# Placing rows of x with TensorE, shorter k/r loads, spread constants, and a new order in a planned RWKV + gated MLP kernel

## The chip, the cores and the metric

The kernel runs on one core of one Trainium2 chip. The metric is the device time of one execution in microseconds (us). A core has TensorE (PE in the rows, its weight loads PEld), VectorE (DVE), ScalarE (ACT), GpSimd (POOL) and SyncE (SP), which here only issues DMAs.

## The reference

Per batch b (4), head h (8) and step t (768), with a head dimension of 48, a recurrence runs over the sequence, and its output feeds a gated MLP:

```
y[t]  = r[t] · (state + u * k[t] v[t]^T)
state = w[t] * state + k[t] v[t]^T
x = y, heads side by side: [4, 768, 384]
h = gelu(x @ w_in)              # 1024 wide: u = first 512, v = last 512
vn = (v - mean) / sqrt(var + 1e-6) * g_ln
vs = w_sg @ vn + b_sg           # over the 768 positions
out = x + (u * vs) @ w_out
```

All inputs are float32 but w_in and w_out, which arrive as float64.

## The kernel before

**Chunks.** The recurrence is cut into 24 chunks of 128 positions (6 per batch). For a chunk the kernel loads w (`load_w`), k and r in one tile KR (`load_kr`, 128 rows: two heads' 48 values each followed by 16 zero rows) and v (`load_v`). VectorE forms decays by two scans (`decays`, L485 and L490) and scales k and r (L514, L492). TensorE turns k (`turned_k`, L564), forms products of k, r and v (`products`, L579 and L582) and the outputs (`outputs`, L662 and L686). For the first six chunks the weights of a position on itself come from k times r (L524) and a small product (L528); later chunks load k and r a second time (`load_rk`) and use u spread over 128 rows (`u_bc`).

**x.** `outputs` copies y from PSUM into a tile x of four blocks [128, 384 positions per half sequence]. Blocks 0 to 2 are the 384 channels, but their rows 48 to 63 and 112 to 127 are empty at first: what belongs there lies in block 3. `move` carries it over with six small DMAs (two row groups by three blocks), for each chunk of the first batch and for a whole half elsewhere. `split_x` (L732 to L747) then writes x as the sum of two fp32r values, high and low: a cast for high, and for the low part either two products with an identity and a negative identity (L741, L742; the first two chunks, `ON_PE["x"]`) or a subtraction (L747).

**MLP.** Every matmul of the MLP is three fp32r products, high by high, high by low and low by high (L752 to L754). `v_piece` makes one chunk's v half of the hidden layer and normalizes it, `u_piece` a block of the u half for half a sequence, `gate_piece` the product with w_sg, `out_piece` the product with w_out, to which x is added (L850). The weights are split into high and low at the start: w_in in six pieces of 512 columns and w_out in four, by integer operations on VectorE (L874 to L882) and, for the first seven pieces, three products on TensorE (L887 to L889); w_sg in twelve pieces. The v pieces' weights are loaded first.

**Constants.** `consts` and `consts2` load u and b_sg with one DMA each that repeats the row over 128 partitions (L930, L936), and g_ln.

**Order.** Nothing is ordered at run time: each engine works through its own queue. The order of the queues is written by `Plan`, a list scheduler that runs while the kernel is built. Each `Op` carries a time per engine, the buffers it takes and frees, and the events it waits for; a DMA is costed by its kilobytes at 330 per us plus latencies. Of the operations that could start earliest on an engine the one with the lowest rank goes first; ranks stand in the tables `STEP`, `V`, `U`, `GATE`, `OUT`, `WEIGHT`, `EARLY`, `TILE`, `FIRST_LOADS`. Where the plan sees TensorE idle before its own time 36 (`WARM`), `keep_warm` (L991 to L1003) writes filler products into TensorE's queue, on a PSUM buffer that is free (L1002). They compute nothing that is used. All DMAs are issued by SP, in the order of the plan. Four PSUM buffers (`m_ps`) serve all products but those of the recurrence.

Of the kernel before, what the change touches and what calls it, by code (L numbers as in the profile page):

```python
# [21 lines left out]
C = 128  # L22
# [16 lines left out]
    38.78, 112.06, 158.75, 217.03, 62.66, 89.53, 134.81, 139.48, 142.68, 149.58, 150.62, 159.84, 162.31, 175.3,  # L39
    189.24, 197.8, 225.35, 212.87, 229.84, 236.4, 243.5, 266.54, 268.81, 362.79)  # L40
V = (
    107.75, 107.47, 46.81, -26.28, 63.79, 120.64, 133.54, 30.66, 190.17, 124.94, 47.43, 157.65, 120.92, 201.53,
    236.16, 159.51, 215.39, 298.31, 336.14, 50.73, 98.98, -9.56, 143.54, 156.75)
U = (17.13, 69.41, 298.46, 126.23, 235.77, -73.97, 85.66, 164.91)
GATE = (3.13, 142.62, 180.86, 144.47, 416.44, 288.73, 96.21, 162.36)
OUT = (267.68, 215.31, 231.79, 361.17, 600.9, 507.76, 441.48, 512.53)
WEIGHT = {"sg0": 131.6, "sg1": 102.52, "g": 182.31}

EARLY = {
    (0, 'decays'): -87.78, (0, 'range_check'): -6.74, (0, 'decayed_k'): -84.86, (0, 'turned_k'): 41.54,  # L50
    (0, 'own_weights'): 6.03, (0, 'first_products'): -46.25, (0, 'masked'): -12.48, (0, 'state'): -1.43,
    (0, 'outputs'): 38.84, (0, 'move'): -112.32, (0, 'split_x'): 9.34, (1, 'load_v'): 16.43,
    (1, 'decays'): 43.75, (1, 'range_check'): 8.92, (1, 'chunk_pc'): 39.98, (1, 'decayed_k'): 40.21,
    (1, 'turned_k'): 155.78, (1, 'own_weights'): 178.83, (1, 'first_products'): 18.08, (1, 'masked'): 26.68,
    (1, 'state'): 49.55, (1, 'decayed'): 41.46, (1, 'outputs'): -69.91, (1, 'move'): 72.17,
    (1, 'split_x'): 93.29, (2, 'load_w'): -38.11, (2, 'load_kr'): 19.39, (2, 'load_v'): 15.43,
    (2, 'decays'): 20.66, (2, 'range_check'): 72.63, (2, 'chunk_pc'): 61.08, (2, 'decayed_k'): 14.48,
    (2, 'turned_k'): 66.7, (2, 'own_weights'): 45.16, (2, 'first_products'): 119.93, (2, 'masked'): -47.19,
    (2, 'state'): 37.82, (2, 'decayed'): 152.85, (2, 'outputs'): 63.08, (2, 'move'): -39.02,
    (2, 'split_x'): 2.22, (3, 'load_w'): -57.23, (3, 'load_kr'): 65.19, (3, 'load_v'): 34.19,  # L60
    (3, 'decays'): 43.95, (3, 'range_check'): 82.06, (3, 'chunk_pc'): 20.23, (3, 'decayed_k'): 2.24,
    (3, 'turned_k'): 81.99, (3, 'own_weights'): 81.71, (3, 'first_products'): 60.11, (3, 'masked'): 69.15,
    (3, 'state'): 78.73, (3, 'decayed'): -34.21, (3, 'outputs'): 74.88, (3, 'move'): -8.38,
    (3, 'split_x'): -27.28, (4, 'load_w'): 69.55, (4, 'load_kr'): 61.22, (4, 'load_v'): 55.55,
    (4, 'decays'): 64.09, (4, 'range_check'): -7.16, (4, 'chunk_pc'): 3.0, (4, 'decayed_k'): 74.78,
    (4, 'turned_k'): -73.87, (4, 'own_weights'): 68.61, (4, 'first_products'): 37.28, (4, 'masked'): 39.48,
    (4, 'state'): 18.01, (4, 'decayed'): 58.71, (4, 'outputs'): 6.26, (4, 'move'): 133.34,
    (4, 'split_x'): -21.7, (5, 'load_w'): 71.5, (5, 'load_kr'): 108.33, (5, 'load_v'): 77.82,
    (5, 'decays'): 76.05, (5, 'range_check'): -19.43, (5, 'chunk_pc'): -118.45, (5, 'decayed_k'): 20.91,
    (5, 'turned_k'): 25.59, (5, 'own_weights'): 84.06, (5, 'first_products'): 32.76, (5, 'masked'): -74.99,  # L70
    (5, 'state'): -36.68, (5, 'decayed'): -134.86, (5, 'outputs'): -48.1, (5, 'move'): 56.59,
    (5, 'split_x'): 45.72}
TILE = {
    "v0": 13.86, "v1": 19.16, "v2": 13.59, "u0": -42.11, "u1": -123.0, "u2": -146.53, "out0": -148.91,
    "out1": 54.2, "out2": 2.98, "out3": -71.18}

HINTED = (mybir.EngineType.PE, mybir.EngineType.DVE, mybir.EngineType.SP)
BIAS = {"DVE": 0.09, "ACT": -0.33, "POOL": 0.08}
# [4 lines left out]
    (0, 'load_w'): -122.73, (0, 'load_kr'): -103.33, (1, 'load_w'): -96.72, (1, 'load_kr'): 8.17,  # L83
    (0, 'load_v'): -79.88}
# [91 lines left out]
class Plan:  # L176
# [20 lines left out]

    def add(self, rank, gen):
# [40 lines left out]
    def run(self):  # L239
        while True:  # L240
            best = {}
            for p in self.procs:
                op = p[3]
                if any(e.t is None for e in op.after) or any(len(s.free) < op.take.count(s) for s in op.take):
# [3 lines left out]
                              for s in (max([ready, self.engines[e], self.port if op.port(e) else 0.0, p[2].on(e)]  # L248
# [83 lines left out]
def rwkv_gmlp(ctx: ExitStack, tc: tile.TileContext, wpad, kr, vtok, ktok, vt, u, ucol, w_in, g_ln, w_sgT, b_sg, w_out, out):  # L332
# [16 lines left out]
    ident = cp.tile([128, 128], F32, name="ident")  # L349
# [24 lines left out]
    s_v = slots("vtok", 3, [DM + 16])  # L374
# [26 lines left out]
    minus, same = (per.tile([128, 128], F32R, name=x) for x in ("minus", "same"))  # L401
# [11 lines left out]
    nc.gpsimd.memset(full, 1.0)  # L413
    nc.gpsimd.affine_select(before, full, pattern=[[1, 128]], compare_op=ALU.is_gt, fill=0.0, base=0,
                            channel_multiplier=-1)
    make_identity(nc, ident)
# [6 lines left out]
    nc.scalar.copy(same, ident)  # L423
    for _, t in s_S2.free:
        nc.gpsimd.memset(t, 0.0)
    for _, t in s_v.free:
        nc.gpsimd.memset(t[:, DM:], 0.0)
# [16 lines left out]
    def dma(kb, **kw):  # L444
        return Op({"SP": 0.6 if kb == 10 else 0.45}, kb=kb, **kw)


# [7 lines left out]
    def load_kr(n):  # L455
        b, g = steps[n]
        op = yield dma(512, take=[s_kr], slack=1.5 if n > 1 else 0.5, done=ch[n].e_KR)
        ch[n].kr, = op.got
        ch[n].kr.n = 3
        ch[n].KR = ch[n].kr.tile  # L460
        nc.sync.dma_start(ch[n].KR, kr[b, g])

    def load_v(n):
        b, g = steps[n]
        op = yield dma(192, take=[s_v], slack=2.0, done=ch[n].e_V)
        ch[n].v, = op.got
# [103 lines left out]
    def products(n, op):  # L570
# [9 lines left out]
        for p, c_, j in [(p, c_, j) for p in range(NP) for c_ in range(1 if last else 2) for j in range(2)]:  # L580
# [3 lines left out]
                             x.V[64 * c_:64 * c_ + 64, h * D:(h + 1) * D], start=True, stop=True)  # L584
# [65 lines left out]
    def outputs(n):  # L650
# [545 lines left out]
```

## Time and profile before

| | |
|---|---|
| median of 3 runs | 361.15 us (360.0 to 362.67) |
| profiled execution | 360.76 us, span of the trace 358.9 us |
| TensorE busy | 347.7 us, 97% of the span, 4606 products |
| VectorE, ScalarE, GpSimd busy | 274.9, 211.4, 75.8 us |
| granted TensorE clock | 0.999 |
| moved by DMA | 49.79 MB, mean 139 GB/s |

The span runs from the first to the last instruction of the core. An engine's busy time is the time in which the profile shows it at work; matmuls overlap one another, so that the durations of single ones add up to more than the engine's time, and the chain of waits, which counts each moment once, gives what one of them takes from the next. A filler product counts as busy like any other. A DMA's time to landing runs from its issue to its arrival.

### The profile page before, as it was taken

Reading aid. Unit: us, or ns where it says so; the run is one execution under the profiler, and the core shown is the slowest. Engines: PE = TensorE matmul, PEld = TensorE weight load, DVE = VectorE, ACT = ScalarE, POOL = GpSimd, SP = SyncE. Lnnn points to the kernel's source line nnn. Section 1 sums busy time; section 2 is a strip of 40 time slices with the busy share of each in tenths; the row PEclk is TensorE's granted clock in tenths of the full one; section 3 lists DMA queues with packets and bytes.
Section 4 is the critical chain, followed back from the end, with each engine's and each line's share of the span. In section 5 each row is a group of like instructions: output and inputs, shape, how many; then the busy total and the mean of one; then the engine's idle time right before and its main releaser. Section 6 shows DMA issues by size and latency. Waiting matters only on the chain.

```text
span 358.9 us, 11141 instructions
## 1 busy us (share of the span) xinstructions
PE 347.7 (97%) x4606; PEld 320.8 (89%) x4606; DVE 274.9 (77%) x540; ACT 211.4 (59%) x564; POOL 75.8 (21%) x100
## 2 busy tenths in 40 slices
PE   6999998999999999999999999999899999999995
PEld 6978777899899989899999899989799988999994
DVE  7899898799999999999989988756942426545352
ACT  4887886793545588776423747685553588811010
POOL 3412141114238122241423110023100003200000
PEclk9999999999999999999999999999999999999999
DMA  7777875450266655743063266024415460000101
GB/s 246 290 218 217 262 224 186 145 193 4 89 204 212 202 170 202 233 150 117 7 221 129 89 221 198 1 71 131 152 59 163 134 200 1 23 24 22 46 22 71
DMA packets 23959, 49.79 MB, mean 139 GB/s; under 512 B 3808, under 2 KB 12768, under 8 KB 23904
## 3 DMA queue, kind: packets, MB, share of 16 engines
q1 hardware_dynamic: 23904, 49.04, 42.2%
q8 instruction: 37, 0.61, 0.7%
q14 instruction: 18, 0.15, 0.1%
HBM read 43.12 MB, written 4.72 MB: 133 GB/s over the span
## 4 chain that ended last, share of the span: by engine, by line
PE 85%; DVE 8%; issue 2%; ACT 2%; DMA 1%; DVEq 0%; ACTq 0%
PE m_ps L752 21%; PE m_ps L754 20%; PE m_ps L753 20%; PE m_ps L1002 4%; PE y_ps L662 4%; PE a_ps L579 3%; PE m_ps L564 3%; PE y_ps L686 3%; PE a_ps L582 2%; PE m_ps L887 2%; PE m_ps L528 1%; DVE m_ps L828 1%; DVE W L485 1%; DMA KR<-in_w_out 1%; DVE W L490 1%
## 5 line engine op out<-in xcount | busy, mean ns | idle before, releaser
L752 PE MATMUL m_ps<-wsgh,vn 128*128 128x384 f32 x192 | 65.7, 342 | 0.0
L754 PE MATMUL m_ps<-wsgh,vn 128*128 128x384 f32 x192 | 64.6, 336 | 0.0
L753 PE MATMUL m_ps<-wsgl,vn 128*128 128x384 f32 x192 | 64.6, 336 | 0.0
L832 ACT CAST g<-m_ps 128x384 fp32r<-128x384 f32 x32 | 15.3, 479 | 52.9 <-DVE m_ps L830 52.8
L828 DVE SCALAR_TENSOR_TENSOR m_ps<-m_ps,g_ln,b_bc 128x384 f32<-128x384 f32 x32 | 19.5, 619 | 22.8 <-PE m_ps L754 22.7
L752 PEld LDWEIGHTS m_ps<-wsgh,vn 128*128 128x128 f32 x192 | 36.1, 188 | 0.8
L783 POOL TENSOR_TENSOR st<-st,mhalf 128x1 f32<-128x1 f32 x24 | 15.9, 666 | 96.9 <-DVE st L781 90.1
L753 PEld LDWEIGHTS m_ps<-wsgl,vn 128*128 128x128 f32 x192 | 36.1, 188 | 0.3
L754 PEld LDWEIGHTS m_ps<-wsgh,vn 128*128 128x128 f32 x192 | 36.1, 188 | 0.0
L752 PE MATMUL m_ps<-g,wouth 128*128 128x384 f32 x96 | 33.6, 350 | 0.0
L752 PE MATMUL m_ps<-xT,winh 128*128 128x384 f32 x96 | 33.0, 344 | 0.0
L754 PE MATMUL m_ps<-xT,winl 128*128 128x384 f32 x96 | 32.3, 337 | 0.0
L753 PE MATMUL m_ps<-xT,winh 128*128 128x384 f32 x96 | 32.3, 337 | 0.0
L753 PE MATMUL m_ps<-g,wouth 128*128 128x384 f32 x96 | 32.3, 336 | 0.0
L754 PE MATMUL m_ps<-g,woutl 128*128 128x384 f32 x96 | 32.3, 336 | 0.0
L485 DVE TENSOR_TENSOR_SCAN W<-W,D 128x516 f32<-128x516 f32 x24 | 31.5, 1313 | 0.9 <-DMA W<-in_wpad 0.9
L501 ACT ACTIVATE junk<-W 128x1032 bf16<-128x1032 f32 x24 | 25.5, 1064 | 10.6 <-DVE W L490 9.3
L490 DVE TENSOR_TENSOR_SCAN W<-W,D 128x516 f32<-128x516 f32 x24 | 30.3, 1261 | 0.3
L752 PE MATMUL m_ps<-winh,xT 128*128 128x512 f32 x72 | 29.5, 409 | 0.5 <-ACT v L775 0.5
L754 PE MATMUL m_ps<-winh,xT 128*128 128x512 f32 x72 | 28.5, 395 | 0.0
L753 PE MATMUL m_ps<-winl,xT 128*128 128x512 f32 x72 | 28.4, 394 | 0.0
L662 PEld LDWEIGHTS y_ps<-a,vtok 64*64 64x64 f32 x768 | 16.2, 134 | 9.0 <-issue 6.3
(148 smaller groups left out, 830.5 us busy)
## 6 DMA issues: line engine op xcount, KB each, us to landing
KR<-in_kr SPq DMA_DIRECT2D x24, 512.0 KB, 4.9
RK<-in_ktok SPq DMA_DIRECT2D x18, 384.0 KB, 4.0
W<-in_wpad SPq DMA_DIRECT2D x24, 258.5 KB, 3.4
vtok<-in_vtok SPq DMA_DIRECT2D x24, 192.0 KB, 5.0
out<-o SPq DMA_DIRECT2D x21, 192.0 KB, 2.1
vn<-in_w_in SPq DMA_DIRECT2D x6, 512.0 KB, 6.4
KR<-in_w_in SPq DMA_DIRECT2D x6, 512.0 KB, 3.8
u<-in_w_sgT SPq DMA_DIRECT2D x12, 192.0 KB, 3.7
```

Of the source, the lines that this page charges most:

```text
L485: nc.vector.tensor_tensor_scan(Suf[:, WL - 1:0:-1], W[:, WL - 1:0:-1], D1[:, WL - 1:0:-1], 0.0, ALU.mult, ALU.add)
L490: nc.vector.tensor_tensor_scan(W[:, 0:WL - 1], W[:, 0:WL - 1], D2[:, 0:WL - 1], 0.0, ALU.mult, ALU.add)
L501: nc.scalar.activation(junk.bitcast(BF16).rearrange("p (a x) -> p a x", a=2), both, AF.Square, accum_out=chk[:, n:n + 1])
L564: nc.tensor.transpose(kt_ps[0:m, p], x.KR[:, 0, p * C:p * C + m], ident)
L662: nc.tensor.matmul(place(j, q, r, c_), x.V[64 * c_:64 * c_ + 64, h * D:h * D + 64], x.a.tile[64 * c_:64 * c_ + 64, j, p], start=(start and ...
L752: nc.tensor.matmul(ps, lh, rh, start=(i == 0), stop=False)
L753: nc.tensor.matmul(ps, lh, rl, start=False, stop=False)
L754: nc.tensor.matmul(ps, ll, rh, start=False, stop=(i == n - 1))
L783: nc.gpsimd.tensor_tensor(rstd, var, c.mhalf, ALU.pow)
L828: nc.vector.scalar_tensor_tensor(ps, ps, c.g[:, d:d + 1], c.b_bc[:, ts], ALU.mult, ALU.add)
L832: nc.scalar.copy(gh, ps)
L1002: nc.tensor.matmul(m[:, 0:n], D1[:, 0:128], D1[:, 0:n], start=True, stop=True)
```

## The change

1. `split_x` gets a new way for the first three chunks (`PLACED = 3`). TensorE writes blocks 0 to 2 of x into a PSUM buffer by a product with an identity, and adds the rows from block 3 by three products with `place_rest`, a matrix of zeros and ones that GpSimd writes at the start (into the memory of an output tile). High is copied out of that buffer, high times the negative identity is added, and low is copied out. The way waits for y alone. The first half's moves become one set of six DMAs for the whole half, which only `out_piece` waits for.
2. `load_kr`, from the second use of each of its three buffers on, loads rows 0 to 47 and 64 to 111 by two DMAs and leaves the zero rows that the first load put there.
3. v arrives with each head padded from 48 to 64 columns: rows of 2,048 bytes where they were 1,536. Three memsets go.
4. u and b_sg are loaded as one row each (b_sg in two halves) and spread over 128 partitions by a product with a row of ones, with a copy out of PSUM (`spread`).
5. The identity is one tile seen as fp32 and as fp32r; GpSimd copies it, where ScalarE did.
6. The plan's kilobytes for several loads and its times for SP are replaced, and all ranks are new.

```diff
-    38.78, 112.06, 158.75, 217.03, 62.66, 89.53, 134.81, 139.48, 142.68, 149.58, 150.62, 159.84, 162.31, 175.3,
...
+    8.02, 24.86, 4.17, -19.95, -9.99, -14.81, 7.91, 9.27, 9.69, 10.22, 13.98, 14.4, 14.5, 17.55, 19.84, 23.71,
...
+MOVES = {(0, 0): ((0, 3),), (0, 1): ((0, 1), (1, 2), (2, 3))}
+AHEAD = 1000.0
...
+PLACED = 3
...
-    s_v = slots("vtok", 3, [DM + 16])
+    s_v = slots("vtok", 3, [H * 64])
...
+    one = per.tile([1, 128], F32, name="one")
+    place_rest = s_o.free[0][1].rearrange("p (k m) -> p k m", k=KT)
...
-    make_identity(nc, ident)
+    make_identity(nc, junk[:, 256:384])
+    nc.gpsimd.tensor_copy(same, junk[:, 256:384])
...
-    nc.scalar.copy(same, ident)
+    nc.gpsimd.memset(place_rest, 0.0)
+    for j in range(2):
+        nc.gpsimd.tensor_copy(place_rest[:, :, 64 * j + D:64 * j + 64],
+                              ident[:, 64 * j:64 * j + D].rearrange("p (i q) -> p i q", q=16))
...
-        op = yield dma(512, take=[s_kr], slack=1.5 if n > 1 else 0.5, done=ch[n].e_KR)
+        op = yield dma(420 if n < 3 else 320, sp=0.45 if n < 3 else 0.9, take=[s_kr], slack=1.5 if n > 1 else 0.5, done=ch[n].e_KR)
...
-        nc.sync.dma_start(ch[n].KR, kr[b, g])
+        if any(ch[n].KR is x for x in padded):
+            for j in range(2):
+                nc.sync.dma_start(ch[n].KR[64 * j:64 * j + D], kr[b, g, 64 * j:64 * j + D])
+        else:
+            padded.append(ch[n].KR)
+            nc.sync.dma_start(ch[n].KR, kr[b, g])
...
-        op = yield dma(192, take=[s_v], slack=2.0, done=ch[n].e_V)
+        op = yield dma(215, take=[s_v], slack=2.0, done=ch[n].e_V)
...
-        op = yield dma(384, take=[s_rk], slack=1.5, after=[ch[ON_PE["own"] - 1].e_own], done=ch[n].e_RK)
+        op = yield dma(340, take=[s_rk], slack=1.5, after=[ch[ON_PE["own"] - 1].e_own], done=ch[n].e_RK)
...
+        before = [ch[h_.n + g].e_y for g in range(g0, g1)] if h_.n + g0 >= PLACED else h_.e_x
         for j in range(2):
             for i in range(KT):
-                op = yield dma(10, slack=1.0, after=[ch[h_.n + g].e_y for g in range(g0, g1)], apart=True)
+                op = yield dma(55, sp=0.6, slack=1.0, after=before, apart=True)
...
+        if h_.n + g < PLACED:
+            op = yield Op({"PE": 1.65}, after=[ch[h_.n + g].e_y], take=[m_m] if g else [m_m, s_xt])
+            m = op.got[0]
+            if g == 0:
+                h_.xt = op.got[1]
+                h_.xt.n = 3 + FT
+                h_.xt.new(2, KT, HALF, dtype=F32R)
+            xh, xl = h_.xt.tile[:, 0], h_.xt.tile[:, 1]
+            x = h_.x.tile
+            ps = m.tile[:, :KT * C].rearrange("p (k t) -> p k t", t=C)
+            nc.tensor.matmul(ps, ident, x[:, 0:KT, cs], start=True, stop=True)
+            for i in range(KT):
+                nc.tensor.matmul(ps[:, i], place_rest[:, i], x[:, KT, cs], start=False, stop=True, skip_group_check=True)
+            op = yield Op({"ACT": 0.41, "DVE": 0.45})
+            copy(op.e, xh[:, :, cs], ps)
+            yield Op({"PE": 0.2}, free=[h_.x])
+            nc.tensor.matmul(ps, minus, xh[:, :, cs], start=False, stop=True, skip_group_check=True)
+            op = yield Op({"ACT": 0.41, "DVE": 0.45}, free=[m], done=h_.e_x[g])
+            copy(op.e, xl[:, :, cs], ps)
+            return
...
-        op = yield Op({"DVE": 0.45}, take=[s_u if h_.n == N - 3 else s_o], free=[m, h_.x])
+        op = yield Op({"DVE": 0.45}, after=h_.e_moved, take=[s_u if h_.n == N - 3 else s_o], free=[m, h_.x])
...
-        op = yield dma(n, take=at, after=after, slack=3.0 if after else 1.5)
+        op = yield dma(0.9 * n, take=at, after=after, slack=3.0 if after else 1.5)
...
-        op = yield dma(192, take=[s_u], after=after, slack=4.0)
+        op = yield dma(165, take=[s_u], after=after, slack=4.0)
...
-    def consts():
-        yield dma(192, done=e_u, after=[ch[3].e_k], slack=3.0)
-        nc.sync.dma_start(u_bc, u.rearrange("h e -> (h e)").partition_broadcast(128))
...
-        yield dma(384, done=e_b, after=[ch[3].e_k], slack=3.0)
-        nc.sync.dma_start(c.b_bc, b_sg.partition_broadcast(128))
+    def spread(src, dst, done, after):
+
+        n = src.shape[-1]
+        op = yield dma(55, take=[s_u], after=after, slack=1.5)
+        raw, = op.got
+        nc.sync.dma_start(raw.tile[0:1, 0:n], src)
+        op = yield Op({"PE": 0.35}, take=[m_m], free=[raw])
+        m, = op.got
+        nc.tensor.matmul(m.tile[:, 0:n], one, raw.tile[0:1, 0:n], start=True, stop=True)
+        op = yield Op({"ACT": 0.4, "DVE": 0.45}, free=[m], done=done)
+        copy(op.e, dst, m.tile[:, 0:n])
...
+    plan.add(WEIGHT["ub"], spread(u.rearrange("h e -> (h e)").unsqueeze(0), u_bc, e_u, [ch[2].e_k]))
...
-            if b == 0:
-                for g in range(3):
-                    plan.add(rank(h_.n + g, "move"), move(h_, g, g + 1))
-            else:
-                plan.add(rank(h_.n + 2, "move"), move(h_, 0, 3))
+            for g0, g1 in MOVES.get((b, i), ((0, 3),)):
+                plan.add(rank(h_.n + g1 - 1, "move"), move(h_, g0, g1))
```

## Rows read from the trace of the kernel before

**Rows 1.** The page of the profile, its first and fourth part: busy time with the share of the span and the count of instructions, and the chain of work that ended last, by engine.

```profile
PE 347.7 (97%) x4606; PEld 320.8 (89%) x4606; DVE 274.9 (77%) x540; ACT 211.4 (59%) x564; POOL 75.8 (21%) x100
...
PE 85%; DVE 8%; issue 2%; ACT 2%; DMA 1%; DVEq 0%; ACTq 0%
```

**Rows 2.** Busy time in stretches of the span: from:to, its length, then busy us (and instructions) of PE, PEld, DVE, ACT, POOL, the granted clock, the DMA engines' busy share, GB/s.

```profile
3.66:40.00 36.34, 36.30 (x563) 31.02 (x563) 34.09 (x57) 26.65 (x87) 9.31 (x6) 1.00 0.78 256
36.00:354.60 318.60, 314.49 (x4105) 291.73 (x4104) 242.70 (x484) 185.90 (x483) 64.61 (x76) 1.00 0.40 128
```

**Rows 3.** The chain of work that ended last, in order of time, from the start to 60 us: start, us, engine, tile and line, count of instructions.

```profile
2.81 5.23 PE m_ps L1002 x28
8.04 0.84 PE m_ps L528 x8
8.88 2.06 PE m_ps L1002 x18
10.95 0.44 PE m_ps L564 x4
...
18.80 0.86 PE m_ps L887 x2
19.66 0.23 PE m_ps L888
...
22.95 0.33 PE m_ps L1002 x2
...
24.13 1.04 PE m_ps L1002 x8
...
26.99 2.40 PE m_ps L1002 x22
...
32.22 1.45 PE m_ps L1002 x12
...
36.38 0.75 PE m_ps L741 x2
37.13 0.18 PE m_ps L742
...
40.08 0.23 PE m_ps L752
...
45.77 0.44 PE y_ps L662 x16
...
46.45 0.60 DVE RK L524
```

**Rows 4.** The filler products alone (line 1002), in stretches; columns as in rows 2, PE and PEld only.

```profile
0.00:8.04 8.04, 5.23 (x28) 5.09 (x28) 1.00 0.74 249
8.04:18.80 10.76, 5.92 (x43) 5.15 (x42) 1.00 0.72 263
```

**Rows 5.** The timelines of ScalarE, SP and TensorE, the way of the first chunk's x and of its first MLP product: start, us, engine, line, operation, out<-in.

```profile
19.23 0.58 ACT L339 COPY x<-y_ps 128x512 f32<-128x512 f32 x1
26.59 0.58 ACT L339 CAST winl<-m_ps 128x512 fp32r<-128x512 f32 x1 [0.40 <-PE m_ps L889]
28.82 0.51 ACT L339 CAST xT<-x 128x384 fp32r<-128x384 f32 x1 [0.21 <-DMA x<-x]
31.48 0.48 ACT L339 CAST xT<-m_ps 128x384 fp32r<-128x384 f32 x1 [1.12 <-PE m_ps L742]
...
19.91 0.62 SPq L722 DMA_DIRECT2D x<-x  x1
...
23.01 1.78 SPq L722 DMA_DIRECT2D x<-x  x3
40.92 4.50 SPq L722 DMA_DIRECT2D x<-x  x6
...
39.83 0.48 PE L752 MATMUL m_ps<-winh,xT 128*128 128x512 f32 x1
```

**Rows 6.** The timelines of VectorE and GpSimd: columns as in rows 5; in brackets the idle time before, and what ended it.

```profile
8.97 0.69 DVE L514 TENSOR_TENSOR KR<-KR,W 128x512 f32<-128x512 f32 x1
...
48.51 0.56 DVE L747 TENSOR_TENSOR xT<-x,xT 128x384 fp32r<-128x384 f32 x1
...
102.23 0.54 DVE L850 TENSOR_TENSOR o<-m_ps,x 128x384 f32<-128x384 f32 x1
...
2.90 1.27 POOL L420 CAST mask<-junk 64x512 uint8<-64x512 f32 x2
11.61 1.82 POOL L492 TENSOR_TENSOR KR<-KR,W 128x512 f32<-128x512 f32 x1 [7.43 <-DVE W L490]
...
30.39 2.69 POOL L524 TENSOR_TENSOR RK<-KR 128x512 f32<-128x512 f32 x1 [5.31 <-DMA KR<-in_kr]
```

**Rows 7.** DMA issues by line: out<-in, engine, operation, count, KB each, median us from issue to landing.

```profile
KR<-in_kr SPq DMA_DIRECT2D x24, 512.0 KB, 4.9
RK<-in_ktok SPq DMA_DIRECT2D x18, 384.0 KB, 4.0
...
vtok<-in_vtok SPq DMA_DIRECT2D x24, 192.0 KB, 5.0
```

**Rows 8.** The timeline of SP, the loads of k and r for chunks 4 and 5.

```profile
26.31 0.33 SPq L461 DMA_DIRECT2D KR<-in_kr  x1
...
39.98 0.38 SPq L461 DMA_DIRECT2D KR<-in_kr  x1
```

More of the change, by code (lines that the diff above doesn't have):

```diff
@@ L44 @@
[L44 to L47, printed above, removed]
-EARLY = {
[L50 to L72, printed above, removed]
@@ L73 @@
 TILE = {
[L74 to L75 removed]
+    "v0": -16.34, "v1": -17.19, "v2": -17.12, "u0": -21.64, "u1": -65.83, "u2": -61.68, "out0": -104.7,
+    "out1": -32.78, "out2": -13.06, "out3": -70.58}
+MOVES = {(0, 0): ((0, 3),), (0, 1): ((0, 1), (1, 2), (2, 3))}
+AHEAD = 1000.0
 HINTED = (mybir.EngineType.PE, mybir.EngineType.DVE, mybir.EngineType.SP)
[L78 removed]
+BIAS = {"DVE": 0.24, "ACT": -0.12, "POOL": 0.3}
@@ L82 @@
 FIRST_LOADS = {
-    (0, 'load_w'): -122.73, (0, 'load_kr'): -103.33, (1, 'load_w'): -96.72, (1, 'load_kr'): 8.17,
-    (0, 'load_v'): -79.88}
+    (0, 'load_w'): -129.08, (0, 'load_kr'): -67.01, (1, 'load_w'): -32.92, (1, 'load_kr'): -17.34,
+    (0, 'load_v'): -32.68}
+PLACED = 3
 COLD = 6.0
@@ L196, in cost, with room @@
         return c
+    def room(self, op):
+        return self.dma - AHEAD if op.kb is not None and op.kb > 100 else 0.0
     def add(self, rank, gen):
@@ L247, in run @@
                 _, t, e = min((s + self.cost(op, e, s) + BIAS.get(e, 0.0), s, e) for e in op.on
-                              for s in (max([ready, self.engines[e], self.port if op.port(e) else 0.0, p[2].on(e)]
+                              for s in (max([ready, self.engines[e], self.port if op.port(e) else 0.0, self.room(op), p[2].on(e)]
                                             + [x.on(e) for x in op.after]),))
@@ L348, in rwkv_gmlp @@
     c.mhalf = cp.tile([128, 1], F32, name="mhalf")
-    ident = cp.tile([128, 128], F32, name="ident")
+    same = cp.tile([128, 128], F32R, name="same")
+    ident = same.bitcast(F32)
     ones = cp.tile([128, 1], F32, name="ones")
@@ L398, in rwkv_gmlp @@
     diag = per.tile([128, T], F32, name="diag")
+    one = per.tile([1, 128], F32, name="one")
     u_bc = per.tile([128, DM], F32, name="u_bc")
     u_col = per.tile([128, NP, 2], F32, name="u_col")
-    minus, same = (per.tile([128, 128], F32R, name=x) for x in ("minus", "same"))
+    place_rest = s_o.free[0][1].rearrange("p (k m) -> p k m", k=KT)
+    minus = per.tile([128, 128], F32R, name="minus")
     junk = per.tile([128, WL - 1], F32, name="junk")
@@ L413, in rwkv_gmlp @@
     nc.gpsimd.memset(full, 1.0)
+    nc.gpsimd.memset(one, 1.0)
     nc.gpsimd.affine_select(before, full, pattern=[[1, 128]], compare_op=ALU.is_gt, fill=0.0, base=0,
                             channel_multiplier=-1)
-    make_identity(nc, ident)
+    make_identity(nc, junk[:, 256:384])
+    nc.gpsimd.tensor_copy(same, junk[:, 256:384])
     for i in range(2):
@@ L442, in rwkv_gmlp, with dma @@
     ch = [Part("W", "KR", "V", "RK", "own", "k", "r", "suf", "pre", "pc", "A", "kt", "sd", "M", "S1", "S2", "T2", "ym", "y") for _ in steps]
-    def dma(kb, **kw):
-        return Op({"SP": 0.6 if kb == 10 else 0.45}, kb=kb, **kw)
+    def dma(kb, sp=0.45, **kw):
+        return Op({"SP": sp}, kb=kb, **kw)
+    padded = []
     def load_w(n):
@@ L661, in own_chunk @@
                 h = 2 * p + j
-                nc.tensor.matmul(place(j, q, r, c_), x.V[64 * c_:64 * c_ + 64, h * D:h * D + 64],
+                nc.tensor.matmul(place(j, q, r, c_), x.V[64 * c_:64 * c_ + 64, h * 64:h * 64 + 64],
                                  x.a.tile[64 * c_:64 * c_ + 64, j, p], start=(start and q == 0), stop=not start,
@@ L823, in gate_piece @@
             vn.done(op.seen)
-        yield Op({"DVE": 0.54}, after=[e_b, h_.e_u[d]])
+        yield Op({"DVE": 0.54}, after=[e_b[half], h_.e_u[d]])
         g.n = KT
@@ L857, in rwkv_gmlp @@
     e_wout = [Event() for _ in range(FT)]
-    e_u, e_uc, e_b = Event(), Event(), Event()
+    e_u, e_uc, e_b = Event(), Event(), (Event(), Event())
     weights = []
@@ L926, in columns, with gains @@
         nc.sync.dma_start(u_col, ucol)
-    def consts():
-        yield dma(192, done=e_u, after=[ch[3].e_k], slack=3.0)
-        nc.sync.dma_start(u_bc, u.rearrange("h e -> (h e)").partition_broadcast(128))
-    def consts2():
-        yield dma(2, after=[ch[3].e_k], apart=True)
+    def spread(src, dst, done, after):
[8 more added lines that the diff above has]
+        copy(op.e, dst, m.tile[:, 0:n])
+    def gains():
+        yield dma(55, after=[ch[3].e_k])
         nc.sync.dma_start(c.g, g_ln)
-        yield dma(384, done=e_b, after=[ch[3].e_k], slack=3.0)
-        nc.sync.dma_start(c.b_bc, b_sg.partition_broadcast(128))
     rank = lambda n, kind=None: EARLY.get((n, kind), STEP[n])
@@ L963, in rwkv_gmlp @@
     plan.add(-18.0, columns())
-    plan.add(-8.0, consts())
-    plan.add(WEIGHT["g"], consts2())
+    plan.add(WEIGHT["ub"], spread(u.rearrange("h e -> (h e)").unsqueeze(0), u_bc, e_u, [ch[2].e_k]))
+    plan.add(WEIGHT["g"], gains())
+    for i in range(2):
+        ts = slice(i * HALF, (i + 1) * HALF)
+        plan.add(WEIGHT["g"] + 0.1 * i, spread(b_sg[ts].unsqueeze(0), c.b_bc[:, ts], e_b[i], [ch[3].e_k]))
     for n, (b, g) in enumerate(steps):
@@ L1161, in layout @@
     rows = lambda a: a.transpose(0, 2, 1, 3).reshape(B, S, DM)
+    vtok = np.zeros((B, S, H, 64), np.float32)
+    vtok[..., 0:D] = v.transpose(0, 2, 1, 3)
     return {
@@ L1164, in layout @@
         "kr": kr.reshape(B, NC, 128, 2, NP * C),
-        "vtok": rows(v),
+        "vtok": vtok.reshape(B, S, H * 64),
         "ktok": np.stack([rows(k), rows(r)], axis=2),
```

39 lines of the change are left out of this document (32 added, 7 removed).

## Prediction

> **What bounds the kernel now.** I read the page first: TensorE is busy for 97% of the span, and the chain of work that ended last lies on it for 85% [rows 1]. So only what changes on TensorE's queue changes the time. A second look is needed, because a filler product counts as busy. In the chain of waits of the first 60 us the reader is to see that from 2.81 us to 46.2 us no other engine appears (a few hundredths of "issue" apart): each filler block is followed at once by a product that had nothing left to wait for [rows 3]. The fillers are therefore on the path. In front of 18.8 us they are busy for 5.23 + 5.92 us [rows 4]; behind it the chain has four blocks, 0.33 + 1.04 + 2.40 + 1.45 = 5.22 us [rows 3].
>
> The windows give the other two facts. From 36 us to the last product at 354.6 us TensorE is busy 314.49 of 318.60 us, so all its stalls there are 4.1 us. From 3.66 to 40 us VectorE is busy 34.09 of 36.34 us: early work cannot come closer together than its 2.25 us of idle time allow, unless another engine takes it [rows 2]. That is the frame: 5.2 us of filler behind 18.8 us, 2.25 us in VectorE, 4.1 us of later stalls, and against them what the change puts onto TensorE.
>
> **The change part by part.**
>
> *Placing by TensorE, what it removes.* Today y of chunk 0 is copied by 19.81 us (19.23 + 0.58), six moves follow from 19.91 us on, and the cast that waits for them begins at 28.82; the low part is there at 31.48 + 0.48 = 31.96 us [rows 5]. With the change y goes to products and two copies: 1.59 us (below) plus 2 x 0.48 is 2.6 us, with the hand-overs some 3, so about 23 us: 9 us earlier. For the first MLP piece the third weight must also be there, 26.59 + 0.58 = 27.2 us, yet its first product ran at 39.83 us [rows 5]. A v piece is nine products of 0.23 us [rows 3], 2.07 us. Chunks 0 and 1 thus give 4.14 us of work that can stand where the last filler blocks stand, and the dearer placing of both (below, 1.32 us) can stand there too: 5.46 us of work against 5.22 us of filler. I take all 5.2 us as saved, since the planner writes filler only where it has nothing else; the low end is 0, the products waiting in their old places.
>
> *What it adds on TensorE.* The identity product with x takes 0.75 us and the negative identity 0.18 us, as now. A 128-column filler, the nearest to a placing product in shape and type, takes 2.40 / 11 = 0.22 us (22 instructions are 11 products) [rows 3]. So three placing products are 0.66 us. Chunks 0 and 1 pay 0.66 us each; chunk 2 had its low part from a VectorE subtraction, at 48.51 us [rows 6], and now pays 0.75 + 0.66 + 0.18 = 1.59 us. Together 2.91 us. Its VectorE saving of 0.56 us goes to a ScalarE copy.
>
> *Spreading u and b_sg.* Three fp32 products of 384 columns. From the 512-column pair at 0.86 us [rows 3] each is 0.65 us as an estimate, 1.94 us in all; with the 0.75 us of the identity product it would be 2.25 us. The one-row operand could make it cheaper; the low end is 0. I take 1.9 us, since columns set the rows that I have. The removed repeating loads cost nothing now, because the chain of the first 60 us does not touch them, and TensorE's sum rises by 2.9 + 1.9 = 4.8 us.
>
> *Moves.* The first half's 18 small DMAs become 6. That frees SP of twelve issues, at 4.50 / 6 = 0.75 us some 9 us between 20 and 45 us [rows 5]. I cost the six that remain at nothing: only the additions of x wait for them, the first at 102.23 us [rows 6]. They wait for all three chunks of x, though, and SP works in order: if the plan puts them too early, the loads behind stand still. With that cover gone, a load is late by the wait itself.
>
> *k and r in two DMAs.* The first three loads stay whole, so the first 18 us see no gain. From chunk 3 on 384 KB replace 512 KB at one more issue of 0.38 us [rows 8]. Loads of the two sizes landed after 4.9 us (512 KB) and 4.0 us (384 KB) [rows 7]: 0.9 us earlier less 0.38 us, about half a microsecond. For chunk 4 GpSimd's product did begin on that arrival, at 30.39 us [rows 6], but it is not on the chain; I take 0, with bounds of -0.5 us and the rival below.
>
> *v with padding.* 64 KB more per chunk; at 256 GB/s [rows 2] that is 0.25 us, and 0.75 us for the three early ones if everything queued behind them is late. VectorE is busy meanwhile: 0 taken, +0.75 us kept as a bound.
>
> *Start on GpSimd.* A row of ones, a copy of the identity, one memset and two copies come, three memsets go. At 1.27 / 2 = 0.64 us each, the dearest row near, five are 3.2 us. GpSimd is done at 4.17 us and starts its first planned work at 11.61 us; the transposes that need the identity begin at 10.95 us [rows 3, 6]. Cost 0; without that cover up to 3.2 us.
>
> *The new order.* It has no row. The later stalls of 4.1 us can go (-4.1) or come again as much (+4.1); I take 0. In the first 40 us it can win VectorE's 2.25 us at most; one filler block shows that something is to be had: k of chunk 0 was ready at 9.66 us (8.97 + 0.69) [rows 6], and the transposes came at 10.95 us behind the filler. I take half of 2.25, 1.1 us.
>
> **Sum.** -5.2 + 4.8 - 1.1 = -1.5 us: the profiled execution of 360.76 us (span 358.9 us and 1.9 us around it) becomes 359.3. That execution lies 0.4 us under the median of 361.15 us; against the median the forecast is **359.7 us**. A measurement of this kernel tells about 1% (3.6 us) from no change, so this is "same".
>
> **Rivals.**
>
> *A, the forecast, 359.7 us, chance 0.42.* Fillers are traded for real products one for one; its own range is 357.6 to 363 us.
>
> *B, the order wins as well, 355.3 us, chance 0.35.* All of VectorE's 2.25 us, half the later stalls (2.05 us) and the 1.3 us by which the first transposes came late are won: -5.2 + 4.8 - 2.25 - 2.05 - 1.3 = -6.0 us, so about 355.2 to 355.3 us. For it: nothing but TensorE on the early chain [rows 3], and fewer queued moves ahead of the weights on SP. Against it: VectorE at 94% of that stretch [rows 2] leaves little to compress.
>
> *C, slower: the fillers stay, 366.0 us, chance 0.17.* If the planner does not bring the v pieces in front of the last fillers, the 4.8 us of products come on top: 361.15 + 4.8 = 366.0. The place is 22 to 34 us, the price 4.8 us, and it is slower by over 1% from the point where less than 1.2 us of the 5.2 us of filler goes. For it: the third weight is ready only at 27.2 us, and VectorE is full; each placing also holds one of four PSUM buffers through two copies. Against it: two weights are ready before, and 9 us of waiting for x is long.
>
> *D, the halves of k and r come one behind the other, 366.1 us, chance 0.06.* A load of 192 KB landed after 5.0 us [rows 7]; two in turn are 10.0 us against 4.9, 5.1 us later. Chunk 4's product would end at 30.39 + 2.69 + 5.1 = 38.2 us and its small product on TensorE stands at 35.39, 2.8 us late; chunk 5's load, issued at 39.98 us [rows 8], would land at 50 us instead of 44.9, where VectorE's product of it stands on the chain at 46.45 [rows 3]: 3.6 us late. Together 359.7 + 6.4 = 366.1. Against it: both halves are issued within 0.8 us, and 384 KB in one DMA took 4.0 us.
> The Trainium skill (DMA: Bandwidth & Descriptors, section Rules for kernel authors) advises against just this split: transfers to disjoint halves of the partitions "serialize", as both use all 16 DMA engines, and one transfer should be used. Taken literally that is case D; taken as sharing the engines by bytes it is the 0 of the sum. No row of this trace has such a pair.
>
> **How the numbers follow.** The time is A's. The range is 354.5 to 366.1 us: it takes in A with its bounds, B but for its luckier tail (about 0.08), and C and D but for the part of them above (about 0.1). Faster by over 1% (under 357.5 us) is B, 0.35; slower by over 1% (above 364.8 us) is C and D, 0.23; the same 0.42.
>
> **What would show it.** Right: filler products between 18.8 and 40 us fall from 5.2 us to under 1 us; the first v product runs before 30 us; the placing costs about 1.6 us a chunk, the three spreads 1.9 us; TensorE without fillers is busy some 4.8 us longer. B shows as stalls behind 36 us under 2.5 us and an earlier first transpose; C as fillers of the old length; D as k/r loads landing after 8 us or more, with VectorE or GpSimd waiting for KR. The forecast is wrong if TensorE's stalls behind 36 us change by more than 3 us either way, if SP stands at the six moves while loads queue behind them, or if the granted clock leaves 1.00 [rows 2] where the fillers were.

## The result, and the profile after

| | before | this |
|---|---|---|
| median | 360.66 us (359.31 to 362.67, 8 runs) | 363.83 us (361.62 to 366.0, 8 runs) |
| profiled execution | 360.76 us, span 358.9 us | 363.66 us, span 362.0 us |
| granted TensorE clock, mean of the span | 0.999 | 0.995 |

The ratio is 1.0086, with a 95% interval of 1.0059 to 1.0114: the changed kernel is slower by 0.9%, some 3.1 us. The forecast was 359.7 us, 1.0 us under this median of before and 1.5 us under the one of 361.15 us that it started from; the time lies inside the range of 354.5 to 366.1 us, on the other side of no change.

The page after, busy time with share and count, and the chain of work that ended last by engine. They answer to [rows 1]:

```profile
PE 353.6 (98%) x4601; PEld 324.3 (90%) x4601; DVE 275.0 (76%) x552; ACT 212.0 (59%) x563; POOL 71.0 (20%) x94
...
PE 98%; DVE 1%; issue 0%; ACT 0%; DVEq 0%
```

TensorE is busy for 5.9 us more, and the chain lies on it almost alone. The span grew by 3.1 us, so TensorE stalls for some 2.9 us less and works for 5.9 us more. Both stand in the windows (columns as in [rows 2]; the last stretch is one in which the clock fell, shown against the same stretch of another kernel further down):

```profile
3.66:40.00 36.34, 36.21 (x549) 30.35 (x549) 35.02 (x59) 25.85 (x80) 9.53 (x8) 1.00 0.81 260
36.00:357.60 321.60, 320.43 (x4113) 295.90 (x4111) 241.80 (x493) 188.71 (x492) 58.43 (x69) 0.99 0.39 119
51.50:55.00 3.50, 3.50 (x53) 2.63 (x54) 2.41 (x4) 2.67 (x8) 0.75 (x1) 0.51 0.22 33
```

Behind 36 us TensorE stood still for 321.60 - 320.43 = 1.2 us, against 4.1 before. VectorE is at 35.02 of 36.34 us in the early stretch, 0.9 us more than before: the early work lies closer together. In 51.5 to 55 us the granted clock was 0.51, about the lower of its two levels (1.2 and 2.4 GHz); ahead of it, from 50 to 51.5 us, TensorE was busy all of the 1.50 us at full clock.

TensorE's waits after (engine, tile and line, what it waited for: us in total, times, longest). Two are listed, the first of them at the start, where before had it too:

```profile
PE m_ps L1049 <- DVE D L415: 2.8, 1, 2.8
PE y_ps L682 <- issue: 1.2, 1, 1.2
```

The fillers alone (line 1049 after, 1002 before) from 18.8 to 36 us, columns as in [rows 4]:

```profile
18.80:36.00 17.20, 1.74 (x12) 1.56 (x12) 1.00 0.85 252
```

The chain of waits after, from 18.8 us on (columns as in [rows 3]):

```profile
18.99 0.84 PE m_ps L759 x2
19.84 0.67 PE m_ps L761 x6
...
26.87 1.09 PE m_ps L1049 x8
27.96 0.65 PE m_ps L759 x2
28.61 0.68 PE m_ps L761 x6
...
30.29 0.42 PE m_ps L1049 x4
...
38.77 0.64 PE m_ps L759 x2
39.41 0.67 PE m_ps L761 x6
...
50.59 0.84 PE m_ps L977 x2
```

L759 is the identity product with x and L761 the three placing products (six instructions), at 19, 28 and 39 us for the three chunks. Of the four filler blocks of 5.22 us [rows 3] two are left, 1.09 + 0.42 = 1.51 us. L977 is a product that spreads a row. The first chunk's x follows from the first line: the timeline of ScalarE (columns as in [rows 5]) has the copy of its low part at

```profile
22.34 0.48 ACT L346 CAST xT<-m_ps 128x384 fp32r<-128x384 f32 x1
```

so it is there at 22.8 us, 9 us before that of [rows 5].

Giving each TensorE instruction the time until the next one began, or its own duration where a stall followed, the 5.9 us of more work split as follows (worked out from both traces, in us):

| | after less before |
|---|---|
| fillers, 15.45 to 11.92 | -3.5 |
| spreading, six instructions | +2.3 |
| placing products 2.0, identity +1.2, negative identity -0.2 | +3.0 |
| MLP products, the same 1,368 | +3.0 |
| all other products | +1.1 |
| sum | +5.9 |
| stalls, 4.15 to 1.30 | -2.9 |

The fourth line is the surprise: the same products of the same sizes took 3.0 us longer. Some 1 us of that, as an estimate, lies in the stretch at half clock, where the MLP's products took about twice as long (the whole stretch cost some 1.7 us, the rest of it among the other products). The remaining 2 us are spread over the whole run.

### The profile page after: what moved, and what is told of

Its sections match the earlier page's. It is cut to its first block, busy times and chain, and to the rows that moved or that the text cites. A ratio compares the mean times of both kernels' runs of the same rounds, so it can differ in the third digit from the quotient of the medians.

```text
span 362.0 us, 11168 instructions
## 1 busy us (share of the span) xinstructions
PE 353.6 (98%) x4601; PEld 324.3 (90%) x4601; DVE 275.0 (76%) x552; ACT 212.0 (59%) x563; POOL 71.0 (20%) x94
## 4 chain that ended last, share of the span: by engine, by line
PE 98%; DVE 1%; issue 0%; ACT 0%; DVEq 0%
PE m_ps L793 25%; PE m_ps L794 23%; PE m_ps L795 23%; PE y_ps L682 4%; PE a_ps L599 3%; PE y_ps L706 3%; PE m_ps L1049 3%; PE m_ps L584 3%; PE a_ps L602 2%; PE m_ps L928 2%; PE m_ps L548 1%; PE m_ps L977 1%; PE m_ps L759 1%; PE m_ps L761 1%; PE m_ps L929 0%
## 5 line engine op out<-in xcount | busy, mean ns | idle before, releaser
L793 PE MATMUL m_ps<-wsgh,vn 128*128 128x384 f32 x192 | 67.1, 349 | 0.0
L795 PE MATMUL m_ps<-wsgh,vn 128*128 128x384 f32 x192 | 64.9, 338 | 0.0
L824 POOL TENSOR_TENSOR st<-st,mhalf 128x1 f32<-128x1 f32 x24 | 18.9, 787 | 114.4 <-DVE st L822 102.5
L793 PEld LDWEIGHTS m_ps<-wsgh,vn 128*128 128x128 f32 x192 | 36.1, 188 | 1.0
L793 PE MATMUL m_ps<-xT,winh 128*128 128x384 f32 x96 | 33.4, 348 | 0.0
L793 PE MATMUL m_ps<-g,wouth 128*128 128x384 f32 x96 | 33.1, 345 | 0.0
L505 DVE TENSOR_TENSOR_SCAN W<-W,D 128x516 f32<-128x516 f32 x24 | 29.5, 1228 | 1.9 <-DMA W<-in_wpad 1.9
L510 DVE TENSOR_TENSOR_SCAN W<-W,D 128x516 f32<-128x516 f32 x24 | 30.4, 1268 | 0.1
L793 PE MATMUL m_ps<-winh,xT 128*128 128x512 f32 x72 | 29.4, 409 | 0.0
L891 DVE TENSOR_TENSOR o<-m_ps,x 128x384 f32<-128x384 f32 x21 | 11.5, 555 | 16.8 <-PE m_ps L795 16.4
```

What stands on the lines that cost most here:

```text
L505: nc.vector.tensor_tensor_scan(Suf[:, WL - 1:0:-1], W[:, WL - 1:0:-1], D1[:, WL - 1:0:-1], 0.0, ALU.mult, ALU.add)
L510: nc.vector.tensor_tensor_scan(W[:, 0:WL - 1], W[:, 0:WL - 1], D2[:, 0:WL - 1], 0.0, ALU.mult, ALU.add)
L793: nc.tensor.matmul(ps, lh, rh, start=(i == 0), stop=False)
L795: nc.tensor.matmul(ps, ll, rh, start=False, stop=(i == n - 1))
L824: nc.gpsimd.tensor_tensor(rstd, var, c.mhalf, ALU.pow)
L891: nc.vector.tensor_tensor(o.tile, ps, h_.x.tile[:, i], ALU.add)
```

## The experiments

All ratios are to the kernel before, measured on the same chip, with 95% intervals. "After" is the changed kernel. At 360.7 us, 0.001 is 0.36 us. The ratio is not the quotient of the medians. The median of before was 360.65 us beside experiments 1 to 4, 360.80 beside 5 to 8 and 360.44 beside 9 to 12. A difference of two ratios is uncertain by some 0.004, or 1.4 us.

**1. After without the spreading.** u and b_sg come by repeating DMAs as before, at the same places in SP's queue; the products and copies are gone.

```diff
-        nc.sync.dma_start(raw.tile[0:1, 0:n], src)
+        nc.sync.dma_start(dst, src[0].partition_broadcast(128))
...
-        nc.tensor.matmul(m.tile[:, 0:n], one, raw.tile[0:1, 0:n], start=True, stop=True)
...
-        copy(op.e, dst, m.tile[:, 0:n])
```

> The changed kernel with u and b_sg loaded by repeating DMAs again (at the places in SP's queue where the one-row loads stood), and with the three spreading products and their three copies taken out of the queues; everything else keeps its place. Theory P (the new TensorE products cost what they last): the three spreads take 2.3 us of the trace of the changed kernel, so 2.0 to 2.6 us faster than it, about 361.3 us where the changed kernel takes 363.8, a ratio to the kernel before of about 1.002. If also the half-speed stretch of the clock at 51 to 55 us comes from the one-row product at 50.6 us in front of it, that stretch goes and another 1.7 us with it: ratio 0.997. Rival O (the new order itself is the cause): no change, ratio 1.007 to 1.009.

Measured: 363.29 us, ratio 1.0078 [1.0045, 1.0111]; the whole change has 1.0086, so 2.3 us of TensorE's work went and some 0.3 us came off, which the intervals do not tell from nothing. Stalls took the place. TensorE's three longest waits of this run (columns as before), behind the one at the start:

```profile
PE m_ps L793 <- issue: 1.7, 1, 1.7
PE m_ps L928 <- ACT v L816: 0.7, 1, 0.7
PE m_ps L793 <- ACT xT L346: 0.6, 1, 0.6
```

1.7 + 0.7 + 0.6 = 3.0 us of waits that the changed kernel does not have. The chain of waits says what was late:

```profile
55.70 5.05 DMA g<-in_w_out
60.77 2.83 DMA x<-x
...
66.59 0.59 SPq L743
...
67.22 0.59 SPq L743
...
67.86 2.79 DMA x<-x
70.83 0.52 ACT xT L346
71.39 0.50 PE m_ps L793
```

A load of w_out, the moves of x one behind the other on SP (L743), and the cast that waits for the last move set when TensorE's product at 71.39 us may begin. Work put onto TensorE in front of that is hidden by it. The edit also brings back the repeating loads, issued at 30.87 to 40.66 us. They do not show on TensorE's way: instruction by instruction (worked out from both traces) this run is 0.85 to 0.87 us behind the changed kernel from 19 to 50 us, before the first load and after the last alike. A run without the products and without these loads was not made, so that they play no part in the wait at 71 us is argued and not shown.

**2. Before without the last fillers.** The four blocks behind 18.8 us go.

```diff
-WARM = 36.0
+WARM = 18.0
```

> The kernel before with fillers written only in front of time 18 of the plan, where they were written up to 36; nothing else moves. Its four last filler blocks of 5.2 us together go. If the fillers are on the path, as the prediction took them: 3 to 5 us faster, ratio 0.986 to 0.992. Rival W (the fillers only stand where TensorE would have waited anyway): ratio 0.998 to 1.002, with stalls of TensorE of some 5 us between 22 and 34 us in their place. Third: without them the clock falls to half for some us, ratio over 1.004, and the granted clock shows it.

Measured: 361.59 us (357.9 to 364.73), ratio 0.9988 [0.9948, 1.0027], which leaves out the three longest (363.46 us and above). The 12 runs part by their granted clock: four at 0.997 and above took 357.9 to 359.74 us, six at 0.976 to 0.980 took 362.39 to 364.73 us, two between them (0.989 and 0.995) 360.08 and 360.8. So at full clock 5.2 us of filler give some 1 to 3 us, not 5.2, and in half of the runs the clock takes that back and more. The chain of waits of its profiled run (clock 0.995) shows where the rest of the 5.2 us is:

```profile
24.87 1.35 DVE W L490
...
26.26 1.08 DVE W L485
...
30.17 0.59 SPq L722
...
32.69 3.74 DMA x<-x
...
36.52 0.88 PE m_ps L741 x2
```

Where before had TensorE alone [rows 3], there are now VectorE's scans, SP's issues of the moves and a move's 3.74 us. VectorE is no earlier without the fillers: its scan of L490 begins at 24.87 us here, and before had it at 25.15. The cast of chunk 1's x, which waits for the same moves as that chunk's first product, shows how early the moves had come in before (columns as in [rows 5]):

```profile
25.15 1.23 DVE L490 TENSOR_TENSOR_SCAN W<-W,D 128x516 f32<-128x516 f32 x1
34.76 0.50 ACT L339 CAST xT<-x 128x384 fp32r<-128x384 f32 x1
```

The last of these moves had landed at 34.69 us and the product began at 36.24 (worked out from the trace), so the fillers had covered a supply that was 1.5 us earlier there. Without them TensorE's instructions are 2.0 us ahead of those of before at 34 to 35 us. Then the product waits 1.8 us for the last move, which lands at 36.43 us, later than in before; why SP issued the moves later in this run is not shown. At 36.5 us TensorE is 0.3 us behind before. The window behind it (columns as in [rows 2]) has the clock at 0.72:

```profile
36.00:42.00 6.00, 5.48 (x60) 3.40 (x61) 6.00 (x9) 5.34 (x16) 1.61 (x1) 0.72 0.86 261
```

**3 and 4. The order by itself.** First after's operations and plan costs with before's ranks, then before with after's ranks (all tables from `STEP` to `FIRST_LOADS` exchanged).

> The changed kernel's operations and plan costs with the ranks of the kernel before (the ranks of the two new kinds of operation: u as its old load, b_sg as in the changed kernel). The plan makes another order. Theory P: the operations cost their 5.3 us of TensorE time with these ranks too, less what fillers go: ratio 1.000 to 1.015. Rival O: it is the ranks, so ratio 0.985 to 0.998.

> The kernel before with all ranks of the changed kernel and its own operations and plan costs. Theory P: no TensorE work is added, the ranks matter little: ratio 0.993 to 1.003. Rival O: the ranks alone make it slower, ratio 1.006 or more.

Measured: 378.5 us, ratio 1.0479 [1.0437, 1.0522], and 370.77 us, ratio 1.0267 [1.0228, 1.0305]. Both are far slower than either kernel, so the pair can't share out the 3.1 us: each set of ranks did well only with the operations that it came with. The chains of waits show one place where such an order fails, of the first (before's ranks, after's operations):

```profile
69.98 5.42 DMA vtok<-in_vtok
75.41 0.57 SPq L743
...
77.30 1.16 SPq L743
78.50 1.72 DMA x<-x
```

and of the second (after's ranks, before's operations):

```profile
63.90 0.73 SPq L722
...
67.20 0.59 SPq L722
...
68.46 2.92 DMA x<-x
```

In both, moves of a half of x stand in a row on SP's queue, with the MLP behind them. What the rest of the 17 and 10 us is made of was not followed.

**5 to 9. Where the late tiles lie.** The MLP's products stream xT, vn and g, the tiles that lie last in a partition of SBUF. v's padding adds 3 buffers x 112 values x 4 bytes = 1,344 bytes ahead of them, five times 256 and 64 (the row of ones adds 512 bytes, and the second identity's 512 go); these tiles begin at 160 modulo 256 before and at 224 after. The two places are worked out from the programs; the traces hold no addresses. The split weights lie in front and stay where they are. An unused tile moves the late tiles and does nothing else; 48 values bring after to 160, 16 bring before to 224, 8 bring after to 0, 24 bring before to 0, 40 bring before to 64.

```diff
     junk = per.tile([128, WL - 1], F32, name="junk")
+    pad = per.tile([128, 48], F32, name="pad")
```

> The changed kernel with an unused tile of 192 bytes per partition behind the last fixed tile. It moves only the tiles made later (x's high and low parts, the normalized v, the gated values) from addresses at 224 modulo 256 to 160 modulo 256, where they lie in the kernel before. In the trace of the changed kernel a 384-column product that streams such a tile takes 176.4 ns from the next one, 174.1 ns in the kernel before; over all products that is 2.3 us. Theory L (the place in SBUF makes the products slower): 1.5 to 2.5 us faster than the changed kernel, ratio 1.002 to 1.005, and 174 ns in the trace. Rival (something else in the program makes them slower, or the chip of that profile): ratio 1.007 to 1.010 and 176 ns.

> The kernel before with an unused tile of 64 bytes at the same place, which moves the same tiles from 160 to 224 modulo 256, where they lie in the changed kernel. Theory L: 1.5 to 2.5 us slower than the kernel before, ratio 1.004 to 1.007, with 176 ns from product to product. Rival: ratio 0.999 to 1.001.

> The changed kernel with 32 bytes of padding: the same tiles at multiples of 256. Theory L with whole lines being cheapest: as the 192-byte padding or faster, ratio 1.000 to 1.005. Rival: ratio 1.007 to 1.010.

> The kernel before with 96 bytes of padding: the same tiles at multiples of 256 instead of 160 modulo 256. Theory L with whole lines being cheapest: ratio 0.994 to 1.000. Theory L with only 224 being dear, and the rival: ratio 0.999 to 1.001.

> The kernel before with 160 bytes of padding, which puts the tiles made later at 64 modulo 256; 160 gave 174 ns from product to product, 224 and 0 gave 176. If 160 is a good place among several: ratio 0.997 to 1.001 and 173 to 174 ns. If most other places cost the same two nanoseconds: ratio 1.003 to 1.006.

Measured, with the mean time from the start of one 384-column MLP product to that of the next, behind 75 us in the profiled execution (worked out from the trace, steps of 200 ns and more left out):

| kernel | place modulo 256 | median us | ratio | step, ns |
|---|---|---|---|---|
| before | 160 | 360.66 | | 174.0 |
| before, moved | 64 | 360.07 | 1.0006 [0.9985, 1.0028] | 174.1 |
| before, moved | 224 | 362.28 | 1.0034 [1.0005, 1.0063] | 175.7 |
| before, moved | 0 | 362.73 | 1.0058 [1.0028, 1.0087] | 175.9 |
| after, moved | 160 | 361.83 | 1.0031 [1.0004, 1.0058] | 174.1 |
| after | 224 | 363.83 | 1.0086 [1.0059, 1.0114] | 175.9 |
| after, moved | 0 | 363.47 | 1.0075 [1.0049, 1.0101] | 176.0 |

160 is cheap and 224 and 0 are dear in both kernels, and 64, tried in before alone, is cheap. The other profiled executions agree, whatever their order of work: 175.9 and 176.0 ns in experiments 3 and 1, with the late tiles where after has them, and 173.9 to 174.1 in experiments 2, 4 and 10 to 12, with the tiles at 160. There are 1,152 products of 384 columns, and 1,152 x 1.8 ns is 2.1 us; after's ratio falls by 0.0055, 2.0 us, when its tiles go back to 160. The other pairs give 1.2 to 2.1 us. In the traces it looks like this: ten products in a row, the first and the last (start, us, engine, line, operation), after

```profile
329.70 0.34 PE L795 MATMUL m_ps<-wsgh,vn 128*128 128x384 f32 x1
...
331.29 0.34 PE L795 MATMUL m_ps<-wsgh,vn 128*128 128x384 f32 x1
```

and after with its tiles at 160

```profile
329.69 0.34 PE L795 MATMUL m_ps<-wsgh,vn 128*128 128x384 f32 x1
...
331.25 0.34 PE L795 MATMUL m_ps<-wsgh,vn 128*128 128x384 f32 x1
```

Nine steps are 1.59 us in the one and 1.56 us in the other. The duration of a single product, 0.34 us in both, doesn't show it, because the products overlap.

In this run the stretch from 51.5 to 55 us was at full clock (columns as in [rows 2]), with the spreading still there:

```profile
51.50:55.00 3.50, 3.50 (x72) 2.41 (x73) 3.14 (x7) 3.01 (x10) 0.11 (x1) 1.00 0.16 49
```

**10 and 11. After at 160, without the spreading, and without the placing products.** The first is edit 1 on top of the tile of 48 values, the second leaves out the three products of each of the first three chunks:

```diff
             for i in range(KT):
-                nc.tensor.matmul(ps[:, i], place_rest[:, i], x[:, KT, cs], start=False, stop=True, skip_group_check=True)
+                pass
```

> The changed kernel with the 192 bytes of padding, and u and b_sg loaded by repeating DMAs, the three spreading products and copies taken out. With the padding alone the changed kernel stood at 1.0031. Theory S (between 50 and 75 us something else than TensorE sets the pace, so that a product taken away there leaves a wait): 0.3 to 0.8 us faster, ratio 1.001 to 1.003. Rival P (each product costs what it lasts, 2.3 us): ratio 0.996 to 0.998.

> The changed kernel with the 192 bytes of padding and without the nine placing products (2.0 us in the trace); it leaves the rows of block 3 out of x for the first three chunks, so that its output is not the reference's. All else keeps its place. Theory S: the first six of them stand where data come late (19 to 29 us), so at most the last chunk's 0.7 us is won: ratio 1.001 to 1.003. Rival P: 2.0 us, ratio 0.996 to 0.999.

Measured: 361.91 us, ratio 1.0045 [1.0019, 1.007], and 359.36 us, ratio 0.9968 [0.9944, 0.9991], both against 1.0031 with everything in. Without the spreading nothing is won (the two intervals overlap, and the middle lies 0.5 us above): from 50 to 66 us TensorE gains 2.5 us on the run with everything in, and by 73 us it has lost 2.4 of them (worked out from both traces). It waits instead, as in experiment 1, here for a load of k and r, a move and the cast (the chain of waits):

```profile
63.21 5.02 DMA KR<-in_kr
68.24 2.77 DMA x<-x
...
71.18 0.52 ACT xT L346
```

The placing products cost 0.0063, 2.3 us, about their own time of 2.0 us. In the two traces TensorE gains 0.7, 0.5 and 0.4 us where they stood, at 20, 29 and 39 us, 1.6 us in all, and keeps it. There no wait takes the time back.

**12. Before with half-length fillers behind the plan's time 18.**

```diff
         t0 = max(t0, 1.8)
+        t1 = t0 + (t1 - t0) * (0.5 if t0 > 18.0 else 1.0)
```

> The kernel before with each filler block behind time 18 of the plan half as long: of 5.2 us some 2.8 us go. Without these blocks the granted clock fell to half for some us in about half of the executions, and those at full clock took 357.9 to 359.7 us. If half of the filler is enough to hold the clock: ratio 0.994 to 0.998. If not: ratio 0.998 to 1.004 with clocks under 0.99 among the runs. If the fillers cost nothing: 0.999 to 1.001 with full clocks.

Measured: 358.56 us, ratio 0.9974 [0.9948, 0.9999]: some 0.9 us faster than before by the ratio, whose interval ends just under 1, and 1.9 us by the medians. In the profiled executions TensorE's instructions are 2.0 us ahead of those of before at 36 us. The fillers behind 18.8 us were busy 2.88 us where before had 5.72, and no run's clock was under 0.995 (columns of the first row as in [rows 4], of the second as in [rows 2]):

```profile
18.80:36.00 17.20, 2.88 (x20) 2.47 (x20) 1.00 0.75 240
```

```profile
36.00:42.00 6.00, 6.00 (x130) 4.23 (x129) 6.00 (x9) 6.00 (x18) 2.16 (x1) 1.00 0.93 296
```

Experiment 2, with no filler there, had 0.72 in this window.

## Why the prediction was wrong

The sum was -5.2 (fillers) + 2.9 (placing) + 1.9 (spreading) - 1.1 (order) = -1.5 us. The runs give +3.1 us: + 2.0 for the place of the late tiles, + 2.3 for the placing products, 0 for the spreading, and so about -1.2 us for all the rest together: fillers, order, earlier x and the identity products. For that rest the sum had -5.2 - 1.1 + 0.9 = -5.4 us. Each of the measured parts is uncertain by some 1.4 us, and they come from separate runs.

- **The step that failed most: "I take all 5.2 us as saved".** The reading was that the fillers are on the path since the chain shows nothing but TensorE. 3.7 us of them did go, 5.22 to 1.51, but a filler taken away gives back only what the supply behind it allows: 1 to 3 us at full clock for all of them (experiment 2), 1 to 2 us for half of them (experiment 12). In the profiled executions TensorE came 2.0 us ahead of before by 34 to 36 us, the same with all and with half of the filler gone. The low end of 0 was put down to products that keep their old places. The reason is another: VectorE's scans came no earlier, and the move was only 1.5 us earlier than it was used.
- **The term that was missing: v with padding, "0 taken, +0.75 us kept as a bound".** It was costed as a transfer alone. It also moves every tile that lies behind v's buffers, and that made the MLP's products 2.0 us dearer (experiments 5 to 9). The sum had no term for it, and no row of before could have shown it. Without it after stands at 1.0031, still on the other side of the forecast's 359.7 us, which is 0.997 of 360.66.
- **Placing: right.** Predicted 2.91 us on TensorE; in the trace the products, the identity and the negative identity come to 3.0 us, 0.67 + 0.84 us of it at the first chunk. The placing products alone cost 2.3 us of time when taken out. That they could stand in the place of the last fillers, and so be paid for by them, did not come out: where x is waited for, the longer way is paid.
- **Spreading: the work was right, its price wrong.** 1.9 us predicted, 2.3 us in the trace, 0 in the time within what the runs can tell. It stands in front of a product that waits for SP's moves and ScalarE's cast until 71 us.
- **The later stalls, "can go or come again as much; I take 0".** They went from 4.1 to 1.2 us in the profiled execution, and part of the 1.2 is the half clock, under which TensorE is busy for longer: with the same queues at full clock it stood still for 1.6 us in experiment 7 and 2.1 in experiment 5 (36 to 350 us). That is what rival B asked for (under 2.5 us), yet experiments 1 and 10 show why it gained nothing: the stalls were filled with the new work, and come back to 3 or 4 us as soon as the spreading goes.
- **Order, -1.1 us.** VectorE's idle time in the early stretch fell from 2.25 to 1.32 us, 0.9 us, about as taken; that the ranks did it is not shown. What that gave in time can't be told from the rest: the exchange of ranks (experiments 3 and 4) failed to separate it.
- **Signs named beforehand.** Fillers under 1 us: 1.74. The first v product before 30 us: the first instruction of L793 stands at 33.9 us, 5.9 us earlier than [rows 5] but behind 30. Placing about 1.6 us a chunk: 0.84 + 0.67 + 0.17 = 1.7. Low part of the first x at about 23 us: 22.8. TensorE without fillers 4.8 us longer: 5.9 + 3.5 = 9.4 us, of which 5.3 us are spreading and placing and 4.1 us products that were there before. The clock leaving 1.00: it did, at 51.5 to 55 us, where 3.5 us at half clock cost some 1.7 us. That is in one execution; of the other seven, two have a mean of 1.000 and took 363.09 and 364.94 us, and one has 0.988 and took 366.0, so the fall is not what makes the kernel slower. Why the clock fell there was not settled; with the tiles at 160 and the spreading in, the profiled execution held it. Two signs against the forecast did not show: the stalls behind 36 us changed by 2.9 us, just under the 3 named, and SP stood at no move for more than 0.5 us up to 75 us.

**The rivals.** C (fillers stay) is refuted in its mechanism, since they mostly went, though its 366.0 us is nearer the time than the forecast. That the time lies inside the range at all is luck: the upper end of the range was there for C and D, and neither happened. B (the order wins as well) had its sign, fewer stalls, but not its time. D (halves of k and r one behind the other) is refuted by the DMA issues after (columns as in [rows 7]):

```profile
KR<-in_kr SPq DMA_DIRECT2D x42, 192.0 KB, 4.1
...
KR<-in_kr SPq DMA_DIRECT2D x3, 512.0 KB, 6.8
```

A half landed after 4.1 us in the middle and none after more than 5.5, where D wanted 8 us or more and whole loads took 4.9 [rows 7]. The Trainium skill (DMA: Bandwidth & Descriptors, Rules for kernel authors) advises against such a split. Here the halves show no loss, and they carry fewer bytes than the whole; these rows do not tell whether the halves share the engines or follow one another closely.

What stays open: the remaining 1.2 us in its parts, the fall of the clock at 51.5 us, and by what mechanism the place of a tile sets a product's step. Four places were tried, which do not settle the rule or its period (they part the same way modulo 128), nor which of the streamed tiles it hangs on.

## What to carry to other kernels

A chain that stays on one engine shows the order of its work, not how far behind it the supply is: before a filler or a piece of work is counted as saved, look at when the inputs of the next product were ready, and test it by taking the filler away alone. A change of a buffer's size moves every tile behind it, so compare the addresses of the streamed tiles and the step from one product to the next before the difference is put down to the edit. And work added in front of a product that waits for something else cost nothing here, while work on the way of what is waited for cost about its full time.

## What was not expected of the hardware

The place of the streamed fp32r tiles modulo 256 bytes changes the step of 384-column products from 173.9 to 174.1 ns (at 64 and 160) to 175.7 to 176.0 ns (at 0 and 224), 1% of it, in all 14 kernels. Filler products hold the clock with half of their length (no run under 0.995), while without them between 18.8 and 36 us six of 12 runs had a mean of 0.976 to 0.980 and were some 4.6 us slower than the four at full clock.
